# Top-k attention and a cosine-gated feed-forward: in the first 28 units, the scores of two units stand ahead of the P@V of two others in TensorE's order

## The chip, the cores and the metric

One core of one Trainium2 chip. The metric is the device time of one execution in microseconds (us); the median of several runs stands for a kernel, and one more execution was taken with the hardware profiler. The core's engines are TensorE (PE: matmuls; PEld: the loading of its weights), VectorE (DVE), ScalarE (ACT), GpSimd (POOL) and SyncE (SP), which here only issues DMAs. Each engine runs its own instructions in program order and waits for others by semaphores.

## The reference

```python
# q, k, v: (8, 8, 576, 64) float32: batch, heads, sequence, head dimension
scores = (1 / sqrt(64)) * q @ k^T                  # 576 x 576 for each batch and head
kth    = 32nd largest score of each row
scores = where(scores >= kth, scores, -1e9)
attn   = exp(scores - max); attn = attn / (sum(attn) + 1e-9)
o      = attn @ v                                  # "P@V" below
x      = o as (8*576, 8*64) = (4608, 512)
h      = x @ w_in                                  # 512 -> 2048
out    = (h * cos(h)) @ w_out                      # 2048 -> 512
```

All of it is float32. The largest part of VectorE's work is the search for the 32 largest of every row of 576 scores.

## The kernel before

**Units.** The 4608 tokens are cut into 36 tiles of 128. A tile has four head pairs, and a unit is one tile with one head pair: 144 units, numbered in order, tile by tile. The sequence of 576 isn't a multiple of 128, so a tile can lie in two batches; its four units then have two parts of 64 rows (units 16 to 19 are the first such), and their score matmuls come as twice as many of half the height.

**Slots.** The loop `for i in range(NU + 1)` writes the program out by hand, one slot for each unit; nothing is reordered later. Slots 0 to 8 are `early_slot`, slots 9 to 140 `slot`, the rest `last_slot`. VectorE's part of slot `i` is the search of unit `i`: first the fold (L247, in `topk_first`), which reads the scores both from PSUM and from a copy in SBUF and makes two half-length rows of them, then four rounds of MAX8 and MATCH_REPLACE8. The other steps of a unit follow in later slots: bounds, mask and exponentials on ScalarE in slot `i+1`; in slot `i+2` the reciprocal of the sum on VectorE (L346), the normalising (L351) and the splitting into 16-bit halves (L363) on GpSimd, then on SP's queue the write of these halves to DRAM (L368) and a transposing DMA that brings P back as `pT` (L374). P@V (`values`, L411) is made in even slots for two units at once, those numbered `i-4` and `i-3`, from `pT` and `v`.

**Scores.** `scored` says in which slot a unit's scores (`scores`, L223) are made. An odd unit's are made one slot ahead of its search. An even unit's are made two slots ahead, together with those of the odd unit in front of it, but for units with two parts, where only the one with head pair 0 goes two slots ahead. So an even slot `i` mostly makes the scores of units `i+1` and `i+2`, and an odd slot none; slot 16 makes only unit 17's, and slot 17 unit 18's.

**PSUM.** The scores of 576 keys don't fit a bank for each head. The first 448 go to `sc`, a tile of two banks with two buffers; a buffer comes free when its unit has been folded. The last 128 of two units, and the results of P@V, share one more tile, `rim`, also of two banks:

```python
rim = ps.tile([P, 2, 512], F32, tag="rim", name="rim", bufs=1)
sc_ends = [rim[:, :, i * (S - SB) : (i + 1) * (S - SB)] for i in range(2)]
room = [rim[:, j, 2 * (S - SB) :] for j in range(2)]
```

`sc_ends[n % 2]` takes the last scores of unit `n`, in both banks; `room[0]`, the second half of the first bank, takes P@V. ScalarE empties them: `take_scores` copies `sc` (L233) and then the unit's part of `rim` (L234) to `s` in SBUF, and `take_values` copies P@V to `xT` (L417), the feed-forward's input. The waits between engines are put in by the language's tile layer, from the tiles that each instruction reads and writes.

**Feed-forward.** `feed(n)` puts up to `n` pieces of the feed-forward between the attention's matmuls: 8 matmuls with `w_in` (L468, tile `mm`) or 2 with `w_out` (L546, tile `o`). Which piece comes next is decided while the program is written, by counts of slots (`tick`, `lag`) and a credit. `take_banks` empties filled banks on ScalarE (L481, L556); the cosine is made on GpSimd (L507 to L516, L533) and ScalarE (L526). The weights are loaded and decoded in the early slots.

**Loads.** `at_slot` says in which slot SP's queue gets the loads of q and k (L188 to L191; five buffers, each free once its last scores are made) and of v (L199, L204; six buffers, each free once its last P@V is made). They stand in the slot behind the row write and the transposing DMA.

Of the kernel before, what the change touches and what calls it, by code (L numbers as in the profile page):

```python
# [31 lines left out]
def kernel(  # L32
# [16 lines left out]
    NP = H // 2  # L49
# [83 lines left out]
    def decode_second(n):  # L133

        for _ in range(min(n, len(wq["second"]))):
            st, w = wq["second"].popleft()
            wi = w.bitcast(I32)
            nc.vector.tensor_scalar(
                out=wi, in0=wi, scalar1=3, scalar2=None, op0=ALU.logical_shift_left
            )  # L140
            nc.vector.scalar_tensor_tensor(
                out=wi, in0=st[:, :, 1], scalar=-(2**31), in1=wi, op0=ALU.bitwise_and, op1=ALU.bitwise_or
            )
            wq["third"].append((st, w))
# [71 lines left out]
    def scores(u):  # L216
        sc = u["sc"] = ps.tile([P, 2, 512], F32, tag="sc", name="sc", bufs=2)
        for to, k0, k1 in ((sc, 0, SB), (sc_ends[u["n"] % 2], SB, S)):
            for j in range(2):
                d = slice(j * D, (j + 1) * D)  # L220
                for b, q0, rows, r0 in u["parts"]:
                    st = pairs[b, u["hp"]]
                    nc.tensor.matmul(  # L223
                        to[r0 : r0 + rows, j, 0 : k1 - k0],
                        st["q"][d, q0 : q0 + rows],
                        st["k"][d, k0:k1],
                        start=True,
                        stop=True,
                    )

    def take_scores(u):
        s = u["s"] = work.tile([P, 2, S], F32, tag="s", name="s", bufs=4)
        nc.scalar.copy(out=s[:, :, 0:SB], in_=u["sc"][:, :, 0:SB])  # L233
        nc.scalar.copy(out=s[:, :, SB:S], in_=sc_ends[u["n"] % 2])  # L234
        if not u["folds"]:
            del u["sc"]
# [23 lines left out]
    def topk_first(u, w):  # L260

        u["top"] = tops[u["n"] % len(tops)]
        merges = [merge_first, merge_second] if w and w["folds"] else []
        if u["folds"]:
            for op in (ALU.max, ALU.min):
                fold(u, op)
                if merges:
                    merges.pop(0)(w)
        else:
            u["rest"] = work.tile([P, 2, S], F32, tag="rest", name="rest", bufs=1)  # L270
        for merge in merges:
            merge(w)
        topk_round(u, 0)

    def topk_round(u, rnd):
        top, rest, lasts = u["top"], u["rest"], TOPK // 8 - 1
        end = TOPK - 1 - 8 * rnd
        at = top[:, :, end : end - 8 if rnd < lasts else None : -1, 0]
        if u["folds"]:
            search(at, rest[:, :, 0:HS], rest[:, :, 0:HS], rnd < lasts)  # L280
            if rnd < TOPK // 16:

                low = top[:, :, 1 + 8 * rnd : 9 + 8 * rnd, 1]
                search(low, rest[:, :, HS:S], rest[:, :, HS:S], rnd < TOPK // 16 - 1)
        else:
            search(at, u["s"] if rnd == 0 else rest, rest, rnd < lasts)
        if rnd == lasts:
            del u["rest"]
# [23 lines left out]
    def bounds(u):  # L312

        ends = u.pop("top").rearrange("p j r i -> p j (r i)")
        ends = ends[:, :, 2 * TOPK - 2 :] if u["folds"] else ends[:, :, 2 * TOPK - 2 :: 2 - 2 * TOPK]
        nb = u["nb"] = small.tile([P, 2, 2], F32, tag="nb", name="nb")
        nc.scalar.mul(out=nb, in_=ends, mul=-SCALE)
        nd = u["nd"] = small.tile([P, 2], F32, tag="nd", name="nd")
        for j in range(2):
            nc.scalar.activation(  # L320
                out=nd[:, j : j + 1], in_=ends[:, j, 1:2], func=AF.Identity,
                bias=nb[:, j, 0:1], scale=SCALE,
            )
# [20 lines left out]
    def reciprocal(u):  # L344
        u["rden"] = small.tile([P, 2], F32, tag="rden", name="rden")
        nc.vector.reciprocal(u["rden"], u.pop("den"))  # L346
# [47 lines left out]
    def values(us):  # L394


        o = room[0]
        for i, u in enumerate(us):
            pT = u.pop("pT")
            for b, _, rows, r0 in u["parts"]:  # L400
                st = pairs[b, u["hp"]]
                r = slice(r0, r0 + rows)
                to = slice(i * P + r0, i * P + r0 + rows)
                for c in range(NT + 1):
                    for j in range(2):
                        d = slice(j * D, (j + 1) * D)
                        if c < NT:
                            lhsT, rhs = st["v"][:, c, d], pT[:, j * (NT + 1) + c, r]
                        else:
                            lhsT, rhs = st["v_tail"][:, d], pT[:, NT, r]  # L410
                        nc.tensor.matmul(o[d, to], lhsT, rhs, start=c == 0, stop=c == NT)  # L411

    def take_values(us):
        blk, hp, n = block_of[us[0]["tok"]], us[0]["hp"], len(us)
        if "xT" not in blk:
            blk["xT"] = work.tile([P, NP, P], F32, tag="xT", name="xT", bufs=5)
        nc.scalar.copy(  # L417
            out=blk["xT"][:, hp : hp + n].rearrange("p h q -> p (h q)"),
            in_=room[0][:, 0 : n * P],
        )  # L420
        blk["left"] -= n
        blk["tick"] = ff["tick"]
# [62 lines left out]
    def take_banks():  # L485
        while full:
            take, *what = full.popleft()
            take(*what)
# [30 lines left out]
    def sines(least):  # L519

        n = sum(c[3] < ff["now"] for c in waiting)
        if n == 0 or (n < least and waiting[0][3] + 2 > ff["now"]):
            return
        for _ in range(n):
            blk, g, x, _, scale = waiting.popleft()
            nc.scalar.activation(out=x, in_=x, func=AF.Sin, bias=halfpi, scale=scale)  # L526
            sined.append((blk, g, x))
# [52 lines left out]
    def feed(n):  # L580

        ff["tick"] += 1
        while n > 0 and ff["credit"] >= 1:
            for kind in (ff["kind"], 1 - ff["kind"]):
                if (can_first, can_second)[kind]():
                    break
            else:
                return
            if kind == 0:
                ff1(*first.popleft())  # L590
            else:
                ff2(*second.popleft())
            if kind != ff["kind"] or ff["half"]:
                ff["kind"], ff["half"] = 1 - kind, 0
            else:
                ff["half"] = 1
            n, ff["credit"] = n - 1, ff["credit"] - 1
# [8 lines left out]
    EARLY, LAST = 2 * NP, NU - NP  # L606
# [9 lines left out]
    for n in range(NP, len(order)):  # L616
        i = last[order[n - 5]] if n >= 5 else 0
        at_slot.setdefault(max(i, NP + 2), []).append((load_qk, *order[n]))
        i = last_values[order[n - 6]] if n >= 6 else 0
# [53 lines left out]
    def slot(i, u, w, x, z):  # L673
        if x:
            reciprocal(x)
        if u:
            topk_first(u, w)
            decode_second(2)
        if u:
            topk_round(u, 1)  # L680
            topk_round(u, 2)
            topk_round(u, 3)
        made = scored.get(i, [])
        if z:
            take_banks()
        feed(1)
        if z:
            values(z)
        for m in made:
            scores(m)  # L690


        late = len(made) > 0

        decoding = i < EARLY + 8
        if i % 2 and not decoding:
            sines(1)
        if w:
            bounds(w)
            mask(w)  # L700
        take_banks()
        if w and late:
            exponentials(w)
        if z:
            take_values(z)
        take_scores(units[i + 1])
        if w and not late:
            exponentials(w)
        load_weights(2)
        if x:  # L710
            normalise(x)
            split(x)
            write_halves(x)
            transposes(x)

        for load, b, hp in at_slot.get(i, []):
            load(b, hp)
        gate(1)
        feed(1 if len(made) == 2 else 2)
        take_banks()  # L720
        decode_third()
        decode_first(2)
        reduce_first()
        reduce_second()
        feed(1 if len(made) == 2 else 3)
        if decoding or i == LAST:
            sines(1)
# [50 lines left out]
    for i in range(NU + 1):  # L778
# [6 lines left out]
        z = units[i - 4 : i - 2] if i % 2 == 0 and EARLY <= i - 4 < LAST else None  # L785
# [53 lines left out]
```

## Time and profile before

| | |
|---|---|
| four runs | 1504.61, 1507.68, 1510.24, 1519.31 us; median 1508.96 |
| the profiled execution | 1514.49 us, of which the span is 1512.7 |
| busy: PE, PEld | 1418.8 us (94%), 1020.7 us (67%) |
| busy: DVE | 1416.8 us (94%) |
| busy: ACT, POOL | 1139.2 us (75%), 1063.9 us (70%) |
| granted TensorE clock, mean | 0.962 |
| DMA | 212.21 MB, mean 140 GB/s |

How to read it: a line of the timeline has the start, the length, the engine, the source line, the operation, what it writes and reads, and how many instructions of the kind were merged; in brackets stands how long the engine sat idle before and what released it. A line of the waits has who waited for whom, the total, the number of times and the longest. A releaser is inferred from semaphore events. Matmuls are pipelined and their ends are modelled, so a fully busy PE need not be at its peak. Idle time of an engine matters only where that engine, or one that waits for it, sets the end.

### The profile page before, as it was taken

Reading aid. Unit: us, or ns where it says so; the run is one execution under the profiler, and the core shown is the slowest. Engines: PE = TensorE matmul, PEld = TensorE weight load, DVE = VectorE, ACT = ScalarE, POOL = GpSimd, SP = SyncE. Lnnn points to the kernel's source line nnn. Section 1 sums busy time; section 2 is a strip of 40 time slices with the busy share of each in tenths; the row PEclk is TensorE's granted clock in tenths of the full one; section 3 lists DMA queues with packets and bytes.
Section 4 is the critical chain, followed back from the end, with each engine's and each line's share of the span. In section 5 each row is a group of like instructions: output and inputs, shape, how many; then the busy total and the mean of one; then the engine's idle time right before and its main releaser. Section 6 shows DMA issues by size and latency. Waiting matters only on the chain.

```text
span 1512.7 us, 30265 instructions
## 1 busy us (share of the span) xinstructions
PE 1418.8 (94%) x10360; PEld 1020.7 (67%) x10360; DVE 1416.8 (94%) x4809; ACT 1139.2 (75%) x2294; POOL 1063.9 (70%) x806
## 2 busy tenths in 40 slices
PE   3577798999999999999999999999999999999999
PEld 3365366777677777777677776777677777777665
DVE  8999988999999999999999999999999999999831
ACT  5777665888788887888788887788788887788651
POOL 2456757777777777777777777777777777777610
PEclk6588889999999999999999999999999999999999
DMA  8442355545655456546654456555655555544200
GB/s 261 133 120 90 94 159 166 136 133 144 183 151 142 132 148 176 165 131 149 179 163 132 130 146 172 165 133 149 180 165 127 139 148 164 148 132 131 74 8 14
DMA packets 371754, 212.21 MB, mean 140 GB/s; under 512 B 321296, under 2 KB 337936, under 8 KB 371600
## 3 DMA queue, kind: packets, MB, share of 16 engines
q1 hardware_dynamic: 366192, 200.63, 47.6%
q10 hardware_dynamic: 5408, 9.65, 1.8%
q8 instruction: 81, 1.33, 0.4%
q14 instruction: 73, 0.60, 0.1%
HBM read 45.09 MB, written 87.29 MB: 88 GB/s over the span
## 4 chain that ended last, share of the span: by engine, by line
POOL 55%; issue 17%; DVE 14%; PE 7%; ACT 4%; DMA 3%; SPq 1%; POOLq 0%; ACTq 0%; DVEq 0%
POOL halves L363 15%; POOL s L351 11%; POOL g L533 9%; POOL x L516 8%; DVE top L307 5%; DVE rest L310 4%; POOL x L508 4%; POOL x L509 4%; POOL x L507 4%; PE o L546 2%; DVE rest L247 2%; PE mm L468 2%; DMA rows<-halves 1%; DMA pT<-rows 1%; PE rim L411 1%
## 5 line engine op out<-in xcount | busy, mean ns | idle before, releaser
L307 DVE MAX8 top<-rest 128x8 f32<-128x288 f32 x1716 | 687.7, 449 | 0.0
L468 PEld LDWEIGHTS mm<-xT,w_in 128*128 128x128 f32 x4608 | 540.3, 193 | 67.6 <-issue 61.5
L546 PE MATMUL o<-w_out,g 128*128 128x512 f32 x1152 | 538.5, 601 | 7.1 <-POOL w_out L151 2.7
L468 PE MATMUL mm<-xT,w_in 128*128 128x128 f32 x4608 | 543.6, 276 | 0.8 <-ACT g L481 0.8
L310 DVE MATCH_REPLACE8 rest<-top,rest 128x288 f32<-128x288 f32 x1144 | 500.2, 445 | 0.0
L351 POOL TENSOR_SCALAR s<-s,rden 128x576 f32<-128x576 f32 x288 | 212.6, 750 | 324.7 <-DVE rden L346 316.7
L546 PEld LDWEIGHTS o<-w_out,g 128*128 128x128 f32 x1152 | 203.1, 191 | 196.1 <-issue 180.5
L363 POOL COPY halves<-s 128x2304 uint16<-128x2304 uint16 x132 | 277.8, 2104 | 13.2 <-DMA rows<-halves 4.9
L247 DVE TENSOR_TENSOR rest<-sc,s 128x576 f32<-128x576 f32 x284 | 213.7, 753 | 30.1 <-ACT s L234 21.8
L337 ACT ACTIVATE s<-s,nd 128x576 f32<-128x576 f32 x288 | 219.9, 764 | 0.8
L329 ACT ACTIVATE s<-s,nb 128x576 f32<-128x576 f32 x288 | 205.4, 760 | 0.0
L411 PEld LDWEIGHTS rim<-pT,v 128*64 128x64 f32 x2560 | 135.4, 142 | 86.1 <-issue 38.7
L411 PE MATMUL rim<-pT,v 128*64 128x128 f32 (+1 forms) x2560 | 164.9, 274 | 30.2 <-DMA pT<-rows 22.0
L223 PE MATMUL sc<-k,q 64*128 64x448 f32 (+1 forms) x640 | 160.7, 604 | 9.6 <-DMA k<-in_k_dram 9.5
L533 POOL TENSOR_TENSOR g<-g,x 128x1024 f32<-128x1024 f32 x68 | 160.9, 2366 | 10.7 <-ACT x L526 7.4
L516 POOL TENSOR_TENSOR x<-g,x 128x1024 f32<-128x1024 f32 x68 | 160.7, 2364 | 5.7
L481 ACT ACTIVATE g<-mm 128x512 f32<-128x512 f32 x144 | 84.4, 587 | 100.1 <-PE mm L468 98.7
L233 ACT COPY s<-sc 128x896 f32<-128x896 f32 x144 | 129.4, 899 | 3.5 <-PE sc L223 3.1
L417 ACT COPY xT<-rim 128x256 f32<-128x256 f32 (+1 forms) x78 | 27.7, 355 | 120.5 <-PE rim L223 103.2
L223 PEld LDWEIGHTS rim<-k,q 64*128 64x128 f32 (+1 forms) x640 | 61.0, 187 | 58.8 <-issue 55.9
L526 ACT ACTIVATE x<-x,halfpi 128x1024 f32<-128x1024 f32 x72 | 82.7, 1150 | 15.8 <-POOL x L516 8.3
L526 ACT ACT_TABLE_LOAD x68 | 87.2, 1283 | 2.0 <-ACT ob L556 0.8
(52 smaller groups left out, 1164.2 us busy)
## 6 DMA issues: line engine op xcount, KB each, us to landing
rows<-halves SPq DMA_DIRECT2D x132, 576.0 KB, 2.8
out_dram<-ob ACTq DMA_DIRECT2D x36, 256.0 KB, 2.8
q<-in_q_dram SPq DMA_DIRECT2D x31, 288.0 KB, 3.8
st<-in_moe_w_in_dram SPq DMA_DIRECT2D x16, 512.0 KB, 5.8
v<-in_v_dram SPq DMA_DIRECT2D x32, 256.0 KB, 3.1
st<-in_moe_w_out_dram SPq DMA_DIRECT2D x16, 512.0 KB, 4.4
k<-in_k_dram SPq DMA_DIRECT2D x31, 144.0 KB, 3.6
k<-in_k_dram SPq DMA_DIRECT2D x32, 128.0 KB, 3.6
```

The lines of the kernel that those rows point to most:

```text
L223: nc.tensor.matmul(to[r0 : r0 + rows, j, 0 : k1 - k0], st["q"][d, q0 : q0 + rows], st["k"][d, k0:k1], start=True, stop=True,)
L247: nc.vector.tensor_tensor(out=u["rest"][:, :, i * HS : (i + 1) * HS], in0=sc[:, :, 0:HS], in1=s[:, :, HS:S], op=op,)
L307: nc.vector.max(to[:, j], src[:, j])
L310: nc.vector.match_replace(rest[:, j], to[:, j], src[:, j], NEG)
L337: nc.scalar.activation(out=s[:, j], in_=s[:, j], func=AF.Exp, bias=nd[:, j : j + 1], scale=1.0, accum_out=den[:, j : j + 1],)
L351: nc.gpsimd.tensor_scalar(out=s[:, j], in0=s[:, j], scalar1=rden[:, j : j + 1], scalar2=1.0, op0=ALU.mult, op1=ALU.mult,)
L363: nc.gpsimd.tensor_copy(out=halves, in_=s.rearrange("p (k h) -> p h k", h=2))
L411: nc.tensor.matmul(o[d, to], lhsT, rhs, start=c == 0, stop=c == NT)
L468: nc.tensor.matmul(mm[:, at : at + w], w_in[f // FC][:, c, (f % FC) * P : (f % FC + 1) * P], blk["xT"][:, c], start=c == 0, stop=c == NC - 1,)
L516: nc.gpsimd.tensor_tensor(out=x, in0=g, in1=x, op=ALU.subtract)
L533: eng.tensor_tensor(out=g, in0=g, in1=x, op=ALU.mult)
L546: nc.tensor.matmul(o, g[:, at : at + P], w_out[f], start=f == 0, stop=f == NF - 1)
```

## The change

In `slot`, where `i` is below `EARLY + 5 * NP` (8 + 20 = 28), the call of `values` is moved behind the calls of `scores`, and on ScalarE `take_values` is moved behind `take_scores`. P@V exists in this function from slot 12 and in even slots, so the slots concerned are 12, 14, ..., 26. From slot 28 on the order is as before.

```diff
         feed(1)
-        if z:
+
+        ahead = i < EARLY + 5 * NP
+        if z and not ahead:
             values(z)
         for m in made:
             scores(m)
+        if z and ahead:
+            values(z)
 ...
         if w and late:
             exponentials(w)
-        if z:
+        if z and not ahead:
             take_values(z)
         take_scores(units[i + 1])
+        if z and ahead:
+            take_values(z)
         if w and not late:
             exponentials(w)
```

## The prediction

> **What bounds the kernel now.** I read the table of stretches first, to see which engine has no slack. Columns: stretch in us, length, busy time and instructions of PE, weight loads, VectorE, ScalarE and GpSimd, granted TensorE clock, DMA share, GB/s.
>
> ```profile
> 100.00:150.00 50.00, 35.11 (x212) 26.78 (x211) 46.55 (x142) 38.82 (x83) 35.49 (x28) 0.80 0.31 96
> 250.00:300.00 50.00, 45.32 (x381) 32.67 (x376) 42.54 (x151) 32.96 (x68) 36.66 (x27) 0.93 0.55 150
> 800.00:1200.00 400.00, 396.91 (x2964) 285.19 (x2963) 396.06 (x1384) 319.99 (x640) 313.11 (x231) 1.00 0.55 150
> ```
>
> From 800 to 1200 VectorE is busy 396.06 of 400: it sets the end, and 1 us of idle it loses early is 1 us of the span. TensorE looks as full, but its work repeats every 18.69 us per two slots (in the timeline the o matmuls behind the scores start at 298.85 and 317.54) against VectorE's 19.02 (folds at 272.42 and 291.44): it gains some 0.35 us per pair. So the question is where VectorE idles within slots 12 to 26. I asked for the waits of VectorE and of TensorE from 180 to 270 (total us, times, longest).
>
> ```profile
> DVE rest L247 <- ACT s L234: 11.2, 2, 7.3
> PE rim L411 <- DMA pT<-rows: 12.2, 2, 7.5
> PE sc L223 <- DMA k<-in_k_dram: 1.8, 1, 1.8
> ```
>
> VectorE waits twice, 11.2 us together, for the second score copy; TensorE waits twice for a transposed P (pT). The timeline joins them. Slot 14 (P@V of units 10 and 11, scores of 15 and 16):
>
> ```profile
> 190.84 1.98 PE L411 MATMUL rim<-pT,v 128*64 128x128 f32 x16 [7.50 <-DMA pT<-rows]
> 193.18 1.87 PE L223 MATMUL sc<-k,q 64*128 64x448 f32 x4
> 195.40 1.40 PE L223 MATMUL sc<-k,q 64*64 64x448 f32 x8
> 197.13 0.37 ACT L417 COPY xT<-rim 128x256 f32<-128x256 f32 x1 [4.88 <-PE rim L223]
> 198.19 0.39 ACT L234 COPY s<-rim 128x256 f32<-128x256 f32 x1
> 198.62 0.76 DVE L247 TENSOR_TENSOR rest<-sc,s 128x576 f32<-128x576 f32 x1 [3.92 <-ACT s L234]
> ```
>
> Unit 11's pT lands at 190.84, scores stand in line behind it, and the fold of unit 15 starts 3.92 us late. Slot 20 (P@V of 16 and 17, scores of 21 and 22):
>
> ```profile
> 254.93 1.12 PE L411 MATMUL rim<-pT,v 128*64 128x64 f32 x16 [4.68 <-DMA pT<-rows]
> 257.26 1.87 PE L223 MATMUL sc<-k,q 64*128 64x448 f32 x4
> 261.44 0.37 ACT L417 COPY xT<-rim 128x256 f32<-128x256 f32 x1 [9.69 <-PE rim L223]
> 262.50 0.39 ACT L234 COPY s<-rim 128x256 f32<-128x256 f32 x1
> 262.92 0.76 DVE L247 TENSOR_TENSOR rest<-sc,s 128x576 f32<-128x576 f32 x1 [7.31 <-ACT s L234]
> ```
>
> P@V ends at 257.26, the scores at 261.3. The L417 copy needs only the P@V columns, yet starts after the scores: a reader of `rim` waits for every earlier write of its banks. That decides what the change can bring.
>
> **The change, part by part.** Nothing is added or removed. In the eight slots 12, 14, ..., 26 TensorE issues 8 to 24 score matmuls ahead of 40 to 80 P@V matmuls, and ScalarE the copies L233 and L234 ahead of L417. VectorE's, GpSimd's and SP's orders are untouched, and no DMA is moved; only what DMAs wait for shifts (q and k loads for scores, now earlier; v loads for P@V).
>
> What the new order still waits for: L233 reads `sc`, so it can run once its scores stand. L234 reads `rim`, which P@V now writes ahead of it in program order; by the L417 row it waits for P@V, and so still for pT. The change therefore doesn't take pT off VectorE's path; it takes off the score matmuls and two copies (L417, L233) that came after it.
>
> Slot 14: P@V ends at 193.2 as before, if it starts at 190.84. Ahead of it, scores of 15 run at 182.0 to 183.3; those of 16 need the `sc` buffer of unit 14, whose fold ends at 186.8. No such long wait is in the trace; the nearest rows show TensorE's weight load released by VectorE in 0.17 to 0.76 us, so I start at 187 and, with the slow matmuls of this slot (1.4 + 0.39 us), end at 188.7; unit 10's P@V (2.4 us slow) ends at 191.1. So unit 11 starts 0 to 0.3 late, P@V ends by 193.5, L234 takes 0.39: 193.9. VectorE is ready at 194.7. Its wait of 3.92 us is gone, with 0.8 us to spare. The exponentials of this slot end at 192.2, so ScalarE covers it.
>
> Slots 15 to 19: VectorE and all that hangs on it (GpSimd's normalising, SP's row writes, the k load that TensorE awaits at 223.1) move 3.9 earlier; TensorE, freed at 193.2 in place of 196.95, moves 3.75. Nothing changes place.
>
> Slot 20, by the old times less 3.92: pT of 17 lands at 251.0, its P@V takes 2.33 us as it did (254.93 to 257.26) and ends at 253.35; L234 ends at 253.8 where it would have ended at 258.97 (262.89 less 3.92). VectorE, ready at 251.8, waits some 2.1 in place of 7.31: 5.15 saved. Bounds: with full-speed matmuls (unit 18's P@V takes 1.22, 275.52 to 276.74) 1.1 more; with an L234 that waited for nothing, the whole 7.31.
>
> Slot 22: TensorE leaves slot 20 at 253.35 in place of 261.31, 7.95 earlier, VectorE is 9.07 earlier, so TensorE has lost 1.1 of its lead. Before, unit 23's copy ended at 281.73 and its fold started at 281.95: 0.2 us of lead. Now P@V (ending at 280.1 less 7.95 = 272.15 to 272.6) is followed by L234 alone, 0.4, in place of L417, L233, L234, 1.45. So it ends at about 273.0, VectorE is ready at 272.85: 0.1 to 0.2 us lost. From there the 0.35 us per pair rebuilds the lead; at slot 28, where the old order returns, unit 29's copy has 1.2 us of lead now, and 0.1 then. By slot 34, where TensorE waits 1.59 us for pT at 391.39, both orders meet.
>
> Slot 12: scores of 14 wait for the fold of 12 (to 163.45), where unit 9's pT came at 161.57. P@V ends at some 167.5 (fast matmuls) to 170.7 (slow) in place of 163.4. What hides this is the wait of the o matmuls for w_out at 170.52 and 172.44, and 5 us of lead at the fold of 13 (copy ended at 170.23, fold at 175.75): nothing on the path. Without that cover it would cost up to 4 us.
>
> Sum: 3.92 + 5.15 - 0.2 = 8.9 us. The profiled execution would go from 1514.49 (span 1512.7, 1.8 around it) to 1505.6. The median of the four runs lies 5.5 below that execution; I take the same saving from it: 1508.96 - 8.9 = **1500.1**.
>
> The Trainium skill's page PSUM — Partial Sum Buffer, section "PSUM bank collisions raise a hardware error", says to guard PSUM by bank and quadrant and not by address, since accesses to different columns of one bank collide too. It speaks against this change's full gain, and the 4.88 and 9.69 us of L417 agree; by it the saving is 8.9, by addresses it would be 10.3.
>
> The page TensorE: Matmul & The Clock Gate, section "What's actually happening", lets the clock fall to half after an idle window of about 3.4 us. The trace shows slowing earlier: after 2.44 us of idle at 161.57 sixteen P@V matmuls took 1.44 us where 1.09 is usual. By the page, an estimate, slot 20's wait (2.4 us then) would leave the clock up and the saving would be 10.0.
>
> **Rivals.** (a) The copy doesn't wait for P@V: 3.92 + 7.31, less a lost lead of some 0.9 us at slot 22 (copy done at 271.6 after ScalarE's exponentials, VectorE ready at 270.7): 10.3 saved, 1498.7. For it: the two halves of `rim` are different columns. Against: the L417 rows.
> (b) Half the gain: slot 20's pT does not follow VectorE. It comes from a chain through k at 223.1, GpSimd's wait for `g` (5.45 us at 229.09) and two row writes (3.6 each). If that chain stays where it is, L234 ends at 257.75 in place of 262.89 and slot 14's gain is swallowed: 5.1 saved, 1503.8. Against: its first link, GpSimd's normalising at 208.17, starts from VectorE.
> (c) Slower: the `sc` buffer takes the place of pT. In slot 14 TensorE now idles from 183.3 to 187, 3.7 us. This decides once pT of 11 lands before 183 (and pT of 17 before 248.6, so that slot 20 has no stall to save): then the old order doesn't stall and the new one gives up 3.7. TensorE's lead at unit 18's fold is 0.6 us (copy ended at 226.56, fold at 227.14), so 3.1 reach VectorE: 1512.1. For it: nothing on VectorE depends on pT, and the runs differ by 15 us. Against: pT of 11 was issued at 186.25 and took 4.6 us, and GpSimd had its halves ready only at 181.7; it can't land before 183 unless GpSimd runs earlier too.
>
> **How the numbers follow.** Forecast 0.58, (a) 0.1, (b) 0.2, (c) 0.07, others 0.05. The four runs spread from 1504.61 to 1519.31, so medians may shift by some 4 us either way: low end, 11.2 saved and 4 lower, 1493.8; high end, 5.1 saved and 4 higher, 1507.9. One per cent, about what a measurement of this kernel can tell from no change, is 15.1 us; even the whole idle time of 11.2 stays under it. Faster by over 1% takes full gain and luck: 0.1; slower by over 1% takes a stall that I don't see: 0.04.
>
> **What would show it.** Right: VectorE's wait at the fold of 15 gone, that of 21 at about 2 us, ending with an L234 just behind P@V; L417 behind L234; a TensorE wait of VectorE in slot 14, some 3 to 4 us; rows after 300 us as before. Wrong: no wait of L234 for P@V (a), a fold of 21 that starts later than 256 (b), or new VectorE idle at slots 18 to 30 (c).

## The result, and the profile after

The changed kernel takes 1506.96 us (median of 54 runs) against 1511.56 for the one before (78 runs, the four shown ahead of the prediction among them). The means, 1507.51 and 1511.45 us, stand in a ratio of 0.9974, 95% interval 0.9966 to 0.9982: 3.9 us (2.7 to 5.1) less. The direction was right, the size less than half of the 8.9 us forecast (by the medians, 4.6 us, just over half). Of the 6.9 us between the forecast time, 1500.1, and the measured median, 2.6 come from the kernel before itself, whose first four runs had a median of 1508.96. One execution further down, the profiled one of not18, took 2410.43 us at a granted clock of 0.554 and is left out of every comparison. The profiled execution of the changed kernel took 1508.73 us, span 1506.9: 5.8 less than the profiled execution of before.

The table of stretches, with the columns that it had before:

```profile
100.00:150.00 50.00, 34.64 (x209) 25.58 (x206) 46.54 (x143) 38.60 (x81) 35.45 (x28) 0.76 0.30 97
250.00:300.00 50.00, 50.00 (x448) 36.50 (x445) 49.79 (x174) 41.37 (x81) 40.29 (x29) 1.00 0.65 159
800.00:1200.00 400.00, 396.19 (x2957) 284.53 (x2956) 395.18 (x1381) 319.24 (x638) 313.90 (x231) 1.00 0.53 149
```

From 250 to 300 VectorE is busy 49.79 us where it was 42.54; its long wait is gone. Before the first changed slot and from 800 on nothing differs that matters. The waits of VectorE and then of TensorE from 180 to 270 (total us, times, longest):

```profile
DVE rest L247 <- ACT s L234: 1.9, 1, 1.9
DVE rden L346 <- ACT den L342: 0.7, 1, 0.7
```

```profile
PE sc L223 <- DVE top L300: 4.8, 1, 4.8
PE sc L223 <- DMA k<-in_k_dram: 3.6, 2, 2.4
```

TensorE no longer waits for pT there at all. It waits 4.8 us for the `sc` buffer, which was foreseen, and 3.6 in place of 1.8 for k, which was not (1.26 in slot 17, 2.38 in slot 18). VectorE lost 11.2 us before and loses 2.6 now: 1.9 at the fold of unit 19 and 0.7 at the reciprocal that stands just ahead of the fold of 20. Slot 14 in the timeline:

```profile
187.31 1.84 PE L223 MATMUL sc<-k,q 64*64 64x448 f32 x8 [4.83 <-DVE top L300]
189.51 1.97 PE L411 MATMUL rim<-pT,v 128*64 128x128 f32 x16
191.69 1.04 PE L411 MATMUL rim<-pT,v 128*64 128x128 f32 x16
192.52 0.88 ACT L233 COPY s<-sc 128x896 f32<-128x896 f32 x1
193.31 0.37 ACT L234 COPY s<-rim 128x256 f32<-128x256 f32 x1
193.57 0.38 ACT L417 COPY xT<-rim 128x256 f32<-128x256 f32 x1
195.10 0.76 DVE L247 TENSOR_TENSOR rest<-sc,s 128x576 f32<-128x576 f32 x1
```

The scores of 16 start when the fold of 14 has ended, P@V follows without a stop, the score copy ends at 193.7 and the fold of 15 starts on time at 195.10. Slot 20:

```profile
250.80 0.69 PE L411 MATMUL rim<-pT,v 128*64 128x64 f32 x16
252.60 0.64 PE L411 MATMUL rim<-pT,v 128*64 128x64 f32 x16
253.40 0.37 ACT L234 COPY s<-rim 128x256 f32<-128x256 f32 x1 [1.19 <-PE rim L411]
253.67 0.38 ACT L417 COPY xT<-rim 128x256 f32<-128x256 f32 x1
254.67 0.76 DVE L247 TENSOR_TENSOR rest<-sc,s 128x576 f32<-128x576 f32 x1
```

No wait for pT and none for the fold of 21. Both old stalls are gone whole. The new one is in slot 18 (P@V of 14 and 15, scores of 19 and 20):

```profile
224.23 0.48 SPq L189 DMA_DIRECT2D k<-in_k_dram  x1
224.31 0.96 PE L223 MATMUL sc<-k,q 64*64 64x448 f32 x2
227.65 1.18 PE L223 MATMUL sc<-k,q 64*64 64x448 f32 x5 [2.38 <-DMA k<-in_k_dram]
229.43 1.86 PE L223 MATMUL sc<-k,q 64*128 64x448 f32 x4
231.65 1.55 PE L411 MATMUL rim<-pT,v 128*64 128x128 f32 x16
234.56 0.37 ACT L234 COPY s<-rim 128x256 f32<-128x256 f32 x1 [4.36 <-PE rim L411]
234.97 0.76 DVE L247 TENSOR_TENSOR rest<-sc,s 128x576 f32<-128x576 f32 x1 [1.92 <-ACT s L234]
```

TensorE reaches the scores of 19 at 224.31, when SP has just issued the load of the k that all but the first two of their matmuls need; it lands at 227.6. Then the matmuls run slow (the four score matmuls take 1.86 us, usually 1.02), P@V comes late, and L234, which waits for P@V, makes the fold of 19 1.92 us late. In the kernel before, P@V stood here and covered that load, as its rows show:

```profile
227.94 0.48 SPq L189 DMA_DIRECT2D k<-in_k_dram  x1
230.02 1.09 PE L411 MATMUL rim<-pT,v 128*64 128x128 f32 x16
232.35 0.98 PE L223 MATMUL sc<-k,q 64*64 64x448 f32 x8
```

### The profile page after: what moved, and what is told of

Read it like the earlier page. It is cut to its first block, busy times and chain, and to the rows that moved or that the text cites. A ratio compares the mean times of both kernels' runs of the same rounds, so it can differ in the third digit from the quotient of the medians.

```text
span 1506.9 us, 30269 instructions
## 1 busy us (share of the span) xinstructions
PE 1419.0 (94%) x10360; PEld 1020.9 (68%) x10360; DVE 1416.9 (94%) x4809; ACT 1139.6 (76%) x2294; POOL 1063.9 (71%) x806
## 4 chain that ended last, share of the span: by engine, by line
PE 40%; POOL 25%; DVE 16%; issue 9%; ACT 5%; DMA 3%; SPq 1%; POOLq 0%; ACTq 0%; DVEq 0%
PE o L546 15%; PE mm L468 14%; POOL halves L363 7%; DVE top L307 6%; POOL s L351 5%; PE rim L411 5%; DVE rest L310 5%; POOL g L533 4%; PE sc L223 4%; POOL x L516 4%; DVE rest L247 2%; POOL x L508 2%; POOL x L509 2%; POOL x L507 2%; DMA pT<-rows 1%
## 5 line engine op out<-in xcount | busy, mean ns | idle before, releaser
L468 PEld LDWEIGHTS mm<-xT,w_in 128*128 128x128 f32 x4608 | 539.5, 193 | 67.5 <-issue 62.3
L468 PE MATMUL mm<-xT,w_in 128*128 128x128 f32 x4608 | 542.8, 276 | 1.1 <-ACT g L481 0.7
```

Source lines behind the costliest of these rows:

```text
L468: nc.tensor.matmul(mm[:, at : at + w], w_in[f // FC][:, c, (f % FC) * P : (f % FC + 1) * P], blk["xT"][:, c], start=c == 0, stop=c == NC - 1,)
```

## Experiments

**How much do the early waits differ between executions?** Four more profiled executions of the kernel before and two of the changed one, each unchanged; two more of the changed one (after_r, after_s) came with the timed runs further down. The expectations weigh two readings of the missing saving. Theory A: the execution that the prediction was worked on had lost more than a usual one. Theory B: the early saving is there and is given back later.

before_2: 

> The kernel before, unchanged: one more profiled execution, to see how far its early waits differ from one execution to the next. Theory A (the profiled execution that the prediction was made against lost more than a usual one): VectorE's idle time at the folds of units 15 and 21 is below 11.2 us, by some 3 us, and the span is about 1509 in place of 1512.7. Theory B (the early waits are the same each time and the saving is given back later): 3.9 and 7.3 us again, span within 1 us of 1512.7.

before_3: 

> As before_2, a third profiled execution of the kernel before. Theory A: idle time of VectorE at folds 15 to 21 differs from 11.2 by some us, and the span with it. Theory B: 11.2 again.

before_4: 

> A fourth profiled execution of the kernel before. If its early waits differ between executions, VectorE's idle time at the folds of 15 and 21 lies between 5 and 11 us (11.2, 7.0 and 11.0 so far), and the time follows: some 1510 with 7 us, some 1514 with 11. If not, 10 to 11 us.

before_5: 

> A fifth one, as before_4: 5 to 11 us at the folds of 15 and 21, and a time that follows it.

after_2: 

> The changed kernel, unchanged: one more profiled execution. Theory A: TensorE's wait for k in slot 18 and VectorE's idle time at the fold of unit 19 (1.9 us) come again, within 1 us, and early idle time of VectorE (folds 15 to 21) is 2 to 3 us. Theory B: the same early, but idle time at the folds behind 300 us comes to 5 us or more, where before has 4.

after_3: 

> As after_2, a third profiled execution of the changed kernel. Theory A: 2 to 3 us of idle time early. Theory B: 5 us or more at the folds behind 300 us.

VectorE's waits from 180 to 300, from the same view as above, in the second execution of before:

```profile
DVE rest L247 <- ACT s L234: 7.0, 2, 3.7
```

| VectorE's idle time, us | executions | mean |
|---|---|---|
| before, folds of 15 and 21 | 11.2, 7.0, 11.0, 6.4, 6.6 | 8.4 |
| changed, fold of 19 and the reciprocal ahead of that of 20 | 2.6, 2.5, 4.9, 2.3, 2.1 | 2.9 |
| before, 300 to 1405 | 4.1, 5.6, 7.2, 7.6, 1.8 | 5.2 |
| changed, 300 to 1405 | 5.6, 5.4, 4.6, 5.5, 4.6 | 5.1 |
| before, span | 1512.7, 1508.8, 1515.4, 1512.7, 1505.6 | 1511.0 |
| changed, span | 1506.9, 1503.9, 1505.3, 1503.5, 1505.3 | 1505.0 |

(The idle times are summed from the timeline.) Each span less its two idle times is 1495.7 to 1498.7 us, so these waits account for the differences between the ten executions to within some 3 us. Theory A holds: the execution that the prediction was worked on lost the most of the five, though a second one lost nearly as much. The fold of 15 is steady (3.1 to 4.5 us late), that of 21 is not (7.3, 3.7, 6.9, 2.0, 3.5). The two high ones go with a later start of GpSimd's L507 behind slot 17: 229.09 and 229.24, against 227.09, 227.84 and 226.93. And they are the two whose TensorE ran at half clock in slot 17. There it had waited 1.81 and 1.85 us for k, against 1.06 to 1.43 in the other three; from 225 to 227 us the granted clock was 0.50 and 0.51, in the three others 1.00. The stretch in the first and the second execution (the clock is the third number from the end):

```profile
225.00:227.00 2.00, 2.00 (x9) 1.53 (x8) 2.00 (x9) 1.31 (x3) 0.00 (x0) 0.50 0.31 68
225.00:227.00 2.00, 2.00 (x15) 1.59 (x14) 2.00 (x9) 1.79 (x4) 0.00 (x0) 1.00 0.58 99
```

With it the `w_in` matmuls (L468) of that slot took 2.67 and 2.46 us, in the three others 2.05; their result goes through ScalarE to L507. No run changes the clock alone, so that it makes the late pT is argued from these rows. Theory B falls: behind 300 us both kernels lose the same. Early, the change saves 8.4 less 2.9, 5.5 us, on these ten executions.

**Is the wait for k in slot 18 what takes the rest?** Theory K of the expectations says so; rival R says that the lead lost there would only come back as a wait for pT in slot 20. The change undone in that slot alone, and, the other way round, the two slots with the old stalls changed alone:

```diff
-        ahead = i < EARLY + 5 * NP
+        ahead = i < EARLY + 5 * NP and i != 18     # not18, not18_2
+        ahead = i in (14, 20)                      # only14_20
```

not18: 

> The changed kernel with the old order in slot 18 alone. Theory K (the saving that is missing is a new wait: in slot 18 the scores of unit 19, moved ahead, reach a k load that has not landed, 2.4 us on TensorE and 1.9 + 0.7 us on VectorE): P@V covers that load again, VectorE's idle at the fold of 19 is below 0.5 us, slot 20 has no stall either, and the time is 2 to 3 us below the changed kernel's. Rival R (the lost lead is conserved): the fold of 19 starts on time, but TensorE then waits for pT in slot 20 and the fold of 21 is some 2 us late, as the prediction had it; the time is within 1 us of the changed kernel's.

not18_2: 

> The changed kernel with the old order in slot 18 alone, for its profile. Theory K: no wait for k in slot 18, VectorE's idle time at folds 19 to 22 below 0.5 us. Rival R: the fold of 19 on time, but TensorE waits 2 to 3 us for pT in slot 20 and VectorE some 2 us at the fold of 21.

only14_20: 

> The new order in slots 14 and 20 alone, where VectorE idled for pT; the old one in the six others. Theory K: the whole saving comes from these two slots, the fold of 19 is on time, and the time is 2 to 3 us below the changed kernel's, near that of not18. Rival S (the other slots bring lead too, since two copies stand ahead of P@V in them): VectorE idles some 1 us more behind slot 22 than in not18, and the time is 1 to 2 us above it.

Measured: not18 at 0.9955 of before (0.9939 to 0.9972), 6.8 us less; this interval overlaps that of the changed kernel, so the time alone decides nothing. The profile of not18_2 (1502.94 us) has no idle time of VectorE over 0.15 us from 180 to 300, and for TensorE in this stretch:

```profile
PE sc L223 <- DVE top L300: 4.8, 1, 4.8
PE sc L223 <- DMA k<-in_k_dram: 1.5, 1, 1.5
PE rim L411 <- DMA pT<-rows: 0.3, 1, 0.3
```

What remains for k is slot 17's wait, which was there before; slot 18's is gone, and of a wait for pT only 0.3 us stands in its place, with no fold late. So K, not R, in this kernel. only14_20 took 0.9963 (0.9946 to 0.9980), 5.6 us less, and its profile shows R after all:

```profile
PE sc L223 <- DVE top L300: 3.7, 1, 3.7
PE rim L411 <- DMA pT<-rows: 3.4, 1, 3.4
PE sc L223 <- DMA k<-in_k_dram: 0.7, 1, 0.7
```

TensorE waits 3.4 us for pT in slot 20, the fold of 21 is 2.0 us late, as the prediction had it, and the reciprocal behind it 1.2. In that execution the row write of unit 16 took 5.2 us until the transposing DMA behind it was issued (232.29 to 237.47), in not18_2 2.8 (233.06 to 235.88). The executions further down that are without slot 18's loss tell this from the choice of slots. With 2.8 to 3.4 us for that write (mid17, mid17_2, all_mid) the pT of unit 17 lands at 248.3 to 248.8 and the fold of 21 is on time; with 4.6 us (all_mid_2, where every slot has the new order) it lands at 250.5 and the stall is back. So the residue goes with the length of that write, not with the slots that are changed; why the write is sometimes longer stays open. only14_20's lower saving against not18 lies within the intervals.

**The same by moving the load.** In place of undoing slot 18, the loads of slot 17 are issued ahead of that slot's transposing DMA; then the same in the kernel before, where nothing should wait for them.

```diff
             write_halves(x)
+            if i == 17:
+                for load, b, hp in at_slot.pop(i, []):
+                    load(b, hp)
             transposes(x)
```

mid17: 

> The changed kernel with the q and k loads of slot 17 issued on SP ahead of that slot's transposing DMA, no longer behind it. Theory K: they are issued some 2.8 us earlier (that DMA's time on SP's queue), k lands before TensorE reaches the scores of 19 or at most 0.5 us after, the fold of 19 is late by less than 0.5 us, and the time falls by 2 to 3 us; pT of 15 lands 2.3 us later, but P@V of 15 starts some 3 us after its old landing. Rival R: TensorE's wait moves to pT (in slot 18 or 20) and the time stays within 1 us.

mid17_2: 

> The changed kernel with the loads of slot 17 ahead of its transposing DMA, beside after_s. Theory K: 2 to 3 us below after_s, no idle time at the folds of 19 to 21. Rival: the same time within 1 us, since another wait follows.

after_s: 

> The changed kernel beside mid17_2 on one chip. Theory K: 4 to 5 us below before, 2 to 5 us idle at the folds of 19 and 20 in its profile.

before_mid17: 

> The kernel before with the q and k loads of slot 17 ahead of that slot's transposing DMA, and nothing else. Theory K: the scores of 19 stand behind P@V there and wait for no load, so the earlier load covers nothing; pT of 15 lands some 2 us later, still ahead of its P@V; time within 1.5 us of before. Rival (the moved loads gain by themselves): 3 us or more below before.

On one chip, after_s took 0.9978 of before (0.9962 to 0.9994) and mid17_2 0.9950 (0.9934 to 0.9966): means of 1510.76 and 1506.40 us, 4.4 us apart; mid17 had 0.9958 (0.9941 to 0.9976). The profile of mid17, slot 18:

```profile
220.18 0.48 SPq L189 DMA_DIRECT2D k<-in_k_dram  x1
224.81 0.56 PE L223 MATMUL sc<-k,q 64*64 64x448 f32 x1 [0.30 <-DMA k<-in_k_dram]
229.51 0.37 ACT L234 COPY s<-rim 128x256 f32<-128x256 f32 x1 [0.42 <-PE rim L411]
```

k is issued 2.5 us ahead of the fold of 18 (222.71), in the changed kernel 0.6 us behind it (224.23 against 223.60); TensorE waits 0.3 us for it, and no fold from 15 to 22 is late, in either execution. before_mid17 took 0.9991 (0.9973 to 1.0009): the moved loads gain nothing that these runs can tell by themselves. So the wait for k in slot 18 (2.2 to 2.4 us of TensorE's time in all five profiles of the changed kernel) is what that kernel loses: 2.1 to 4.9 us of VectorE's time in these profiles, and 4.4 us between the two means. The profiled executions of mid17 and mid17_2 don't show the gain in their spans (1504.8 and 1507.5 us): VectorE idles 8.1 and 10.0 us behind 300 us there (9.7 in before_mid17), against 4.6 to 5.6 in the changed kernel's five. Whether the moved loads have a part in that, so few profiles don't say; the gain in time rests on the timed runs.

**ScalarE's part of the change.** TensorE's order as changed, the P@V copy ahead of the score copies as before:

```diff
-        if z and not ahead:
+        if z:
             take_values(z)
         take_scores(units[i + 1])
-        if z and ahead:
-            take_values(z)
```

pe_only: 

> TensorE's order changed as in the changed kernel, ScalarE's left: the P@V copy stands ahead of the two score copies. If the score copies' end follows P@V's end, as the prediction has it (a reader of the rim tile waits for all earlier writes of its banks), each new-order slot's score copies end some 1.1 us later behind P@V than in the changed kernel (0.37 for the P@V copy, 0.8 for the copy of sc that could no longer run during P@V): VectorE idles some 1 us more at the fold of 19, and at folds 21 to 27, where the lead is under 1 us, up to 0.5 more; 1 to 2 us above the changed kernel. Rival (the copy of a unit's last scores doesn't wait for P@V, and only TensorE's order counts): the P@V copy then holds the score copies back by the whole of P@V, and it is 2 us or more slower.

after_r: 

> The changed kernel once more, timed beside the two others of this call, so that they can be compared on one chip. Theory K: 4 to 5 us below before; the profile again with the k wait in slot 18 (1.8 to 2.4 us on TensorE) and 2.5 to 5 us of VectorE's idle time at the folds of 19 and 20.

On one chip pe_only took 0.9973 of before (0.9957 to 0.9988) and after_r, the changed kernel, 0.9968 (0.9950 to 0.9986); means of 1509.75 and 1508.68 us. The difference is 1.1 us, within the spread of the runs, so the times don't show it; the profile does. In slot 18 of pe_only:

```profile
236.16 0.37 ACT L417 COPY xT<-rim 128x256 f32<-128x256 f32 x1 [6.95 <-PE rim L411]
236.42 0.91 ACT L233 COPY s<-sc 128x896 f32<-128x896 f32 x1
237.22 0.39 ACT L234 COPY s<-rim 128x256 f32<-128x256 f32 x1
237.64 0.76 DVE L247 TENSOR_TENSOR rest<-sc,s 128x576 f32<-128x576 f32 x1 [4.56 <-ACT s L234]
```

From the end of P@V (236.1) to the end of L234 (237.6) pass 1.5 us; in the changed kernel 0.4 to 0.5 (234.5 to 234.9). The two copies are worth 1.1 us in a stalled slot, as the prediction had it; at the other folds from 15 to 31 this profile has no idle time.

**The new order everywhere.** First with nothing else, then with the loads moved in the four slots that stand to each other as slot 17 does:

```diff
-        ahead = i < EARLY + 5 * NP
+        ahead = True                               # all_slots, all_mid, all_mid_2
```
```diff
             write_halves(x)
+            if i % 36 == 17:                       # all_mid, all_mid_2
+                for load, b, hp in at_slot.pop(i, []):
+                    load(b, hp)
             transposes(x)
```

all_slots: 

> The new order in every slot that makes P@V, 12 to 140. If what a stalled slot loses is the scores and two copies that stand behind P@V, the waits behind 300 us (5 us at four to six folds, each after a TensorE wait for pT of 1 to 2 us) shrink to under 1 us, and the time is 4 us below the changed kernel's. Rival: scores that run ahead reach k loads or the sc buffer too soon in late slots as they do in slot 18, VectorE idles there instead, and the time is the changed kernel's or above.

all_mid: 

> The new order in all slots from 12 on, and the q and k loads of slots 17, 53, 89 and 125 (one sequence pair apart) ahead of the transposing DMA. Theory K: both kinds of waits are covered, VectorE's idle time between the folds of 15 and 140 falls to under 1.5 us, and the time is 5 us or more below the changed kernel's. Rival: as the loads stand ahead, that slot's pT lands 2 us later and TensorE waits for it in slots 18, 54, 90, 126; VectorE loses 1 to 2 us at each and the time stays that of the new order in all slots.

all_mid_2: 

> all_mid once more, on another chip where that is given. Some 1499 us, 1.0% below before; VectorE's idle time between the folds of 15 and 140 below 1.5 us again.

all_slots took 0.9962 of before (0.9948 to 0.9977), no more than the changed kernel's ratio within the intervals. From 300 to 1400 TensorE no longer waits for pT, where the changed kernel has seven waits, 8.7 us; it waits for k instead (2.9 us), and VectorE with it:

```profile
DVE rest L247 <- ACT s L234: 2.9, 3, 1.2
DVE rden L346 <- ACT den L342: 2.1, 3, 0.7
```

Three times, 343 us (36 slots) apart, the picture of slot 18 comes again. With the loads moved too, all_mid shows for the same stretch:

```profile
DVE rden L346 <- ACT den L342: 0.6, 1, 0.6
DVE rest L247 <- DVE rden L346: 0.4, 1, 0.4
```

It took 0.9897 of before (0.9876 to 0.9918; 5 runs) and, on another chip, 0.9925 (0.9907 to 0.9944; 6 runs): medians of 1498.71 and 1501.39 us, 11 to 16 us less than before. It beats both kernels. In the second run's profile slot 20 still had a wait for pT (2.95 us) and the reciprocal behind the fold of 21 came 2.3 late, so the early part isn't clean in each execution.

## Why the prediction was right or wrong

**Right: the mechanism, and rival (a) is out.** L234 waits for P@V (4.36 us at 234.56, 1.19 at 253.40), though it reads other columns of `rim`; the scores and two copies are what the change takes off the path. The rule of the Trainium skill's page PSUM — Partial Sum Buffer, section "PSUM bank collisions raise a hardware error", to guard by bank and not by address, and the trace agree here; the rows can't tell a wait by bank from one by tile, since `rim` is a single tile.

**Right: slot 14.** P@V was put to end by 193.5 and L234 at 193.9, with 0.8 us to spare; it was 193.7 for L234, and the fold started on time. The wait for the `sc` buffer was put at 3.7 us and was 4.83: TensorE came at 182.5, not at 183.3.

**Right: slot 12.** Its scores waited 3.21 us for the fold of 12, and the copy of unit 13 ended at 170.35, where it had ended at 170.23: nothing on the path.

**Wrong: "Slots 15 to 19: ... Nothing changes place."** This step failed. It moved all times by 3.9 us but forgot that in slot 18 the scores also move by the length of P@V. Its own rows held a part of the answer. k was issued at 227.94; less 3.9, that is 224.0, and with the 3.6 us that such a load takes (median to landing) 227.6. The scores of 19 would start at 230.02, where P@V started, less 3.9, 226.1, and reach the matmuls that need k 1.0 later: a wait of 0.5 us was to be read off. It was 2.38, with slow matmuls behind it, and cost VectorE 2.1 to 4.9 us. The rest of the wait comes from the flat 3.9: TensorE came to slot 18 5.7 us earlier (224.31). In the execution before, its matmuls behind slot 17's wait for k ran at a granted clock of 0.65 and 0.50 (223 to 225 and 225 to 227 us), in the changed kernel at 1.00 (218 to 224), and from that wait's end to slot 18 passed 6.9 us there and 5.3 here.

**Wrong in a way that partly pays: slot 20.** A residue of 2.1 us was forecast and the changed kernel has none. That VectorE comes 2.6 us later there, by slot 18's loss, isn't needed for it: not18_2, mid17, mid17_2 and all_mid are without that loss and have none either. Their pT of unit 17 lands at 248.3 to 249.1, where the prediction had 251.0; in only14_20 and all_mid_2 it lands at 250.8 and 250.5, and a residue is there (2.0 us and 1.2 at the reciprocal; 0.3 and 2.3). The 251.0 was one execution's time, 254.9, moved by 3.9; the five executions of before have 252.2 to 254.9. It depends on the row writes ahead of pT, as rival (b) suspected; but pT of 17 did follow VectorE (issued at 245.17, 250.62 before), and the fold of 21 started at 254.67, ahead of (b)'s 256, so (b) as it stood is wrong. Slot 22, put at 0.2 us lost, lost nothing.

**Wrong: "I take the same saving from it".** This step failed too, and by as much. The profiled execution lost 11.2 us at the two folds, the mean of five is 8.4; the four runs' median, 5.5 us below that execution, was the hint, and it was used for the level only. Within the profiled pair the early idle time fell by 8.6 us, from 11.2 to 2.6, close to the 8.9 forecast. That is luck: the loss in slot 18, which was not foreseen, is about as large as the losses in slots 20 and 22 that were foreseen and didn't come. (The spans of this pair differ by 5.8 us only; the changed kernel's has 1.5 more idle time behind 300 us.) On the means, the forecast 11.2 less 2.3 became 8.4 less 2.9: a saving of 5.5 us; the timed 3.9 (2.7 to 5.1) is a little below that, which five executions of each kernel don't separate. The table shows no saving given back later (5.2 and 5.1 us). Rival (c) didn't come.

**The clock.** The prediction took slow matmuls from a 2.44 us wait in the trace, against the idle window of about 3.4 us that the Trainium skill's page TensorE: Matmul & The Clock Gate, section "What's actually happening", names. After 2.38 us of idle, with two matmuls just ahead, the granted clock from 229.4 to 231.6 was 0.50, and after 1.81 us in slot 17 of the kernel before it was 0.50 too: the trace was the better guide. No length of wait decides it, though: after 2.17 us at 383.61 in the changed kernel the clock stayed at 1.00.

## What to carry to other kernels

When instructions are moved ahead on an engine, look up for each of their inputs when it lands and what the old order did meanwhile: work that is moved behind may have been the cover of a load. A saving read from one profiled execution is that execution's; where the runs spread by as much as the forecast, profile several executions before a wait that ends in a transfer is counted at its full length. And a stall that goes in one slot is worth a look at every slot built like it: the gain lay in doing the order everywhere together with the loads that it uncovers.

## What the runs showed of the hardware

A TensorE wait of 1.8 to 2.4 us can be enough for the granted clock to fall to 0.50: it did after 1.81 us (slot 17 of before) and 2.38 us (slot 18 of the changed kernel), and didn't after 2.17 us (383.61 us of the changed kernel). In slot 18 the low clock lasted some 3.4 us, an estimate from three stretches:

```profile
227.60:229.40 1.80, 1.75 (x14) 0.84 (x14) 1.80 (x7) 1.65 (x6) 1.80 (x2) 0.95 0.00 0
229.40:231.60 2.20, 2.20 (x9) 1.18 (x8) 2.20 (x9) 0.80 (x1) 2.14 (x3) 0.50 0.00 0
231.60:234.00 2.40, 2.40 (x36) 2.35 (x36) 1.45 (x6) 0.00 (x0) 2.03 (x3) 0.79 0.16 63
```

And one kind of transfer varied more than expected: from the issue of a row write to that of the transposing DMA behind it 2.8 to 5.2 us passed for the same unit 16 (not18_2, only14_20), which is the size of the stalls that this change is about.
